# Attention and a maxout MoE on one core: states transposed by DMA, half of the weights multiplied pair by pair, and an earlier state transpose

## The chip, the cores and the metric

The kernel runs on one core of a Trainium2 chip. The metric is device time in microseconds (us). Before the change three runs gave 148.19, 148.46 and 148.90; the median is 148.46 us.

## What is computed

There are B = 8 batches of H = 8 heads, S = 512 positions of x, Ns = 32 states and D = 64. Attention runs both ways between x and the states; its output is one row per position (4352 rows, 512 wide), and each row goes through a maxout layer.

```python
scores = scale * x @ state.T                 # per batch and head: 512 x 32
xread  = softmax(scores) @ state             # 512 x 64
sread  = softmax(scale * state @ x.T) @ x    # 32 x 64
rows   = concat([xread, sread])              # all heads side by side: 544 x 512 per batch
h1, h2 = rows @ w1, rows @ w2                # 512 -> 1024
out    = maximum(h1, h2) @ w_out             # 1024 -> 512
```

Inputs and output are float32; the products are made in bfloat16.

## The kernel before, in words

**The algebra.** max(h1, h2) is relu(h1 - h2) + h2. So the kernel forms wd = w1 - w2 (`w_sub`) and wwo = w2 @ w_out (`w_wo_mm`, `w_wo_h_mm`), and since xread is the attention weights times the states, it multiplies the states of each batch by wd and wwo first: SW[b] = state x [wd, wwo] (`sw_mm`, `sw_two_mm`, `sw_h_mm`). A batch's rows are then relu(a x SW) x w_out plus a x SW: `l1_mm` and `l1_ev` (L1), `l2_f` and `l2_open` (L2), with `l2_out` copying to the output tile.

**The state matrices.** sbd holds, per batch, the states of head pairs as block-diagonal columns (4 pairs, 64 partitions for each of two heads). To fill it, states are cast to bf16 and transposed. Batches 0 and 1 have their own loads and transposes on TensorE (PE): `state_mm` (L132), then `state_ev` (two copies). Batches 2 to 7 share one load of 256 KB twice (`load_states`), one cast on GpSimd (POOL) into sbr (`states_cast`), eight PE transposes into one PSUM bank (`states_mm`, L157), and two copies of 64x768 (`states_ev`, one on ScalarE (ACT), one on VectorE (DVE)). A second way, `states_dma`, was in the file and was not called.

**Attention of a batch.** x is cast to xo (with a column of ones) and transposed to xt, for batch 0 in four head pairs (`cast_pair`, `xt_pair_mm`, `xt_pair_ev`), from batch 2 on by a DMA transpose of another cast xb (`cast_half`, `xt_dma`). Scores go through exp on ACT to e, DVE sums e to es and takes the reciprocal er (`reduce_pair`, `norm_sums`), and `norm_mul` (L294) multiplies e by er to give a, for one half (two of the four head pairs) at a time. `at_mm` (L317) transposes a on PE to aT for batches 0 and 1; from batch 2 on this is a DMA transpose. `sread_mm` makes the other direction.

**The weights.** w1, w2 and w_out are loaded in four pieces of 256 columns; piece 0 comes in two halves (`load_h`). On the way to wwo each piece of w2 is cast (`w2_cast`), transposed on PE (`w2_tr_mm`) and copied to w2t; each piece of w_out is cast to wo (`wo_cast`, `wo_cast_h` for the halves of piece 0). w1 halves are cast by `w1_cast_h`. The load of w2 piece 3 reuses the buffer of piece 0, and so waits for piece 0's subtraction.

**The order.** The kernel is under a manual schedule: each engine runs its instructions in the order in which the program writes them (lines 617 to 849), so that a waiting instruction holds up all behind it on its engine. Batch 0's attention, the weights' preparation, batch 0's L1 and L2 in parts, and batch 1's attention are interleaved by hand there; a loop over batches 1 to 7 follows, in which batch b's L1 and L2 run while batch b+1's attention is prepared. `idle(n)` (L572) issues n matmuls of 128x256 on a tile of zeros whose result nobody reads. SP issues nearly all DMAs, in written order. PSUM has two pools of four banks, pa and ps, of which a step gets a bank as its argument says.

**The steps around the change.** POOL's order before, in batch 0's part: cast of x pair 2, `state0_neg`, w2 half 0, `norm_mul(0,0)`, wo half 0 (line 648), w1 half 1 (line 655), `w_sub(0)` (line 671, L540), wo half 1 (line 677), w2 piece 1, wo piece 1. PE's order there: idle(15), transposes of x pair 0, idle(3), `state_mm(0)`, transposes of x pair 1, idle(3), scores of pair 0 and so on (lines 617 to 689). Around batch 1's end the lines are 786 to 836.

Of the kernel before, what the change touches and what calls it, by code (L numbers as in the profile page):

```python
# [15 lines left out]
def kernel(  # L16
# [9 lines left out]
    nc = tc.nc  # L26
    B, H, S, D = x.shape
    _, _, Ns, _ = state.shape
# [27 lines left out]
    def copy(eng, o, i):  # L56
        if eng == "A":
            nc.scalar.copy(o, i)  # L58
        elif eng == "V":
            nc.vector.tensor_copy(o, i)  # L60
        else:
            nc.gpsimd.tensor_copy(o, i)  # L62
# [61 lines left out]
    P = {}  # L124
# [5 lines left out]
    def state_mm(b, pool=None):  # L130
        p = P["st", b] = bank(BF16, pool)
        nc.tensor.transpose(p[:, 0:128], sb0[:, b], ident)  # L132
# [18 lines left out]
    def states_cast(eng):  # L151
        copy(eng, sbr.rearrange("p m j d -> p j m d"), sfr.rearrange("p j (m d) -> p j m d", m=8))

    def states_mm(pool=None):
        p = P["st"] = bank(BF16, pool)
        for m in range(8):
            nc.tensor.transpose(p[:, m * 128:(m + 1) * 128], sbr[:, m].rearrange("p j d -> p (j d)"), ident)  # L157

    def states_dma():
        P["st"] = xio.tile([128, NC * 256], BF16, tag="xb", name="stt")  # L160
        nc.sync.dma_start_transpose(out=P["st"].rearrange("p (m r) -> p m r", m=8), in_=sbr.rearrange("p m j d -> p (m j d)"))

    def states_ev(j, eng):
        o = sbd[64 * j:64 * j + 64, 2:B, :, 32 * j:32 * j + 32].rearrange("p b k (l m) -> p (b k) l m", l=4)
        copy(eng, o, P["st"][64 * j:64 * j + 64, :].rearrange("p (m k l) -> p k l m", m=8, l=4)[:, 8:])


    def cast_half(b, g, eng):
        if b not in st:
            st[b] = dict(xb=xio.tile([128, NC, H * D], BF16, tag="xb", name="xb"))  # L170
        copy(eng, st[b]["xb"][:, :, 256 * g:256 * g + 256].rearrange("p c (i d) -> p i c d", i=4),
             xf_t[b][:, 4 * g:4 * g + 4, :].rearrange("p i (c d) -> p i c d", c=NC))
# [15 lines left out]
    def cast_pair(b, k, eng, m=1):  # L188
        xo = st[b]["xo"]
        for j in range(k, k + m):  # L190
            copy(eng, xo[:, :, j, 2:130].rearrange("p c (i d) -> p i c d", i=2),
                 xf_t[b][:, 2 * j:2 * j + 2, :].rearrange("p i (c d) -> p i c d", c=NC))

    def xt_pair_mm(b, k, pool=None):
        d = st[b]
        if "xt" not in d:
            d["xt"] = at.tile([128, NC, 4, 128], BF16, tag="xt", name="xt")
        p = P["xt", k] = bank(BF16, pool)
        for c in range(NC):
            nc.tensor.transpose(p[:, c * 128:(c + 1) * 128], d["xo"][:, c, k, 2:130], ident)  # L200
# [11 lines left out]
    def scores_pair_mm(b, k, pool):  # L212
        d = st[b]
        if "e" not in d:
            att_tiles(b)
        p = P["sc", k] = bank(F32, pool)
        for c in range(NC):
            nc.tensor.matmul(p[:, c * 64:c * 64 + 64], d["xt"][:, c, k, :], sbd[:, b, k, :],
                             start=(c == 0), stop=(c == NC - 1))
# [10 lines left out]
    def xt_dma(b):  # L230
        d = st[b]
        d["xt"] = at.tile([128, NC, 4, 128], BF16, tag="xt", name="xt")
        nc.sync.dma_start_transpose(out=d["xt"].rearrange("p c k t -> p (c k) t"),
                                    in_=d["xb"].rearrange("p c m -> p (c m)"))
# [39 lines left out]
    def scores_ev(b, hh):  # L274
        ev = st[b]["e"].rearrange("p g c i n -> p (g c) i n")[:, :, 2 * hh:2 * hh + 2, :]
        nc.scalar.activation(out=ev.rearrange("p (g c) i n -> p g c (i n)", g=2),  # L276
                             in_=P["sc", hh].rearrange("p (c g m) -> p g c m", c=NC, g=2), func=ACTF.Exp, scale=scale)
# [5 lines left out]
    def norm_sums(b, hh, sums=True):  # L283
        d = st[b]
        if sums:
            ev = d["e"].rearrange("p g c i n -> p (g c) i n")[:, :, 2 * hh:2 * hh + 2, :]
            nc.vector.tensor_reduce(d["es"][:, hh], ev, axis=mybir.AxisListType.X, op=ALU.add)  # L287
        nc.vector.reciprocal(d["er"][:, hh], d["es"][:, hh])

    def norm_mul(b, hh, eng):  # L290
        d = st[b]
        ev = d["e"].rearrange("p g c i n -> p (g c) i n")[:, :, 2 * hh:2 * hh + 2, :]
        av = d["a"].rearrange("p g c i n -> p (g c) i n")[:, :, 2 * hh:2 * hh + 2, :]
        (nc.gpsimd if eng == "P" else nc.vector).tensor_mul(  # L294
            av, ev, d["er"][:, hh].unsqueeze(3).to_broadcast([128, 2 * NC, 2, Ns]))

    def norm(b, hh, eng, sums=True):
        norm_sums(b, hh, sums)
# [13 lines left out]
    def at_mm(b, g, pool=None):  # L312
        if b not in AT:
            AT[b] = keep.tile([128, 2, NC, 128], BF16, tag="at", name="aT")
        p = P["at", g] = bank(BF16, pool)
        for c in range(NC):
            nc.tensor.transpose(p[:, c * 128:(c + 1) * 128], st[b]["a"][:, g, c].rearrange("p i n -> p (i n)"), ident)  # L317

    def at_ev(b, g, eng):
        copy(eng, AT[b][:, g].rearrange("p c t -> p (c t)"), P["at", g][:, 0:512])  # L320
# [43 lines left out]
    def sw_ev(b, lo, hi, g, eng):  # L364
        copy(eng, SW[b][:, g, lo:hi], P["sw", b, lo][g][:, 0:hi - lo])
# [70 lines left out]
    def l2_open(b, c, p, start, stop):  # L436
        for g in range(2):
            nc.tensor.matmul(p, AT[b][:, g, c, :], SW[b][:, g, FF:WC], start=(start and g == 0), stop=(stop and g == 1))  # L438
# [6 lines left out]
    def l2_out(b, c, p, eng):  # L445
        if b not in OB:
            OB[b] = big.tile([128, NC, DM], F32, tag="ob", name="ob")
        copy(eng, OB[b][:, c, :], p)
# [62 lines left out]
    def w1_cast_h(j, eng):  # L511
        copy(eng, w1b[:, :, 128 * j:128 * j + 128], w1f[0][:, :, 128 * j:128 * j + 128])

    def wo_cast_h(j, eng):
        copy(eng, wo[:, j, :], wof[0][:, j, :])
# [23 lines left out]
    def w_sub(q, i0, i1, eng):  # L539
        (nc.gpsimd if eng == "P" else nc.vector).tensor_sub(  # L540
            wd[:, i0:i1, q * FQ:(q + 1) * FQ], w1f[q][:, i0:i1], w2f[q][:, i0:i1])
# [12 lines left out]
    def w_wo_h_mm(i, j, pool=None):  # L554
        if j == 0:
            P["wwo", 0, i] = bank(F32, pool)
        nc.tensor.matmul(P["wwo", 0, i], w2t[:, j, i, :], wo[:, j, :], start=(j == 0), stop=(j == 1))
# [10 lines left out]
    def idle(n, cols=256):  # L568
        if idle_p[0] is None:
            idle_p[0] = bank(F32, pa)  # L570
        for j in range(n):
            nc.tensor.matmul(idle_p[0][:, 0:cols], wz[:, 0:128], wz[:, 0:cols], start=True, stop=True)  # L572

    def l2_part(q, c):
        if ACC[c] is None:
            ACC[c] = bank(F32, pa)
        l2_f(0, c, ACC[c], (2 * q, 2 * q + 1), q == 0, False)
# [39 lines left out]
    idle(15)  # L617
    cast_pair(0, 0, "V")
    copy("A", sb0[:, 0], sf0[:, 0])
    xt_pair_mm(0, 0, pa)  # L620
    cast_pair(0, 1, "V")
    idle(3)
    state_mm(0, None)
    xt_pair_ev(0, 0, "V")
    xt_pair_mm(0, 1, pa)
    cast_pair(0, 2, "P")
    xt_pair_ev(0, 1, "V")
    state_ev(0, "A")
    idle(3)
    scores_pair_mm(0, 0, pa)  # L630
    cast_pair(0, 3, "V")
    xt_pair_mm(0, 2)
    xt_pair_ev(0, 2, "V")
# [11 lines left out]
    xt_pair_ev(0, 3, "A")  # L645
    idle(1)
    scores_pair_mm(0, 2, None)
    wo_cast_h(0, "P")
    scores_pair_ev(0, 2)
    reduce_pair(0, 2)  # L650
    idle(5)
    scores_pair_mm(0, 3, pa)
    scores_pair_ev(0, 3)
    w2_tr_h_mm(0)
    w1_cast_h(1, "P")
    w1_cast_h(0, "A")
    idle(3)
    sread_mm(0, pa)
# [1 line left out]
    sw_h_mm(0, pa)  # L660
    reduce_pair(0, 3)
    norm_sums(0, 1, False)
    norm_mul(0, 1, "V")
    w2_tr_h_ev(0, "A")
    sw_ev(0, 0, 128, 1, "A")
    idle(4)
    w_wo_h_mm(1, 0)
    at_mm(0, 0, pa)
    sw_ev(0, 0, 128, 0, "A")
    at_mm(0, 1)  # L670
    w_sub(0, 0, 4, "P")
    w_wo_h_mm(3, 0)
    w2_cast_h(1, "A")
    at_ev(0, 1, "V")
    sw_h_mm(1, pa)
    sw_ev(0, 128, 256, 1, "V")
    wo_cast_h(1, "P")
    w2_tr_h_mm(1)
    at_ev(0, 0, "A")
    l1_mm(0, 0)  # L680
# [103 lines left out]
    scores_mm(1, 1)  # L784
    l2_part(2, 2)
    states_cast("P")
    scores_ev(1, 0)
    cast_half(2, 0, "P")
    scores_ev(1, 1)
# [3 lines left out]
    sw_ev(0, FF, WC, 0, "A")  # L793
    norm_sums(1, 0)
    norm_mul(1, 0, "P")
    l2_part(3, 2)
    l2_part(3, 1)
    l2_part(3, 3)
    sw_mm(1, FF, WC)
    norm_sums(1, 1)  # L800
    sw_ev(1, FF, WC, 0, "A")
    sread_mm(1)
    norm_mul(1, 1, "P")
    l2_open(0, 3, ACC[3], False, True)
    l2_open(0, 2, ACC[2], False, True)
    l2_out(0, 3, ACC[3], "A")
# [1 line left out]
    at_ev(1, 0, "A")  # L808
    sw_ev(1, FF, WC, 1, "V")
    at_mm(1, 1)  # L810
    cast_half(2, 1, "P")
    sread_norm(1)
    states_mm()
    states_ev(1, "A")
    at_ev(1, 1, "V")
    cast_xo(2)
    l2_out(0, 2, ACC[2], "V")
    l2_open(0, 0, ACC[0], False, True)
    l2_open(0, 1, ACC[1], False, True)
    states_ev(0, "V")  # L820
    l2_out(0, 1, ACC[1], "A")
    l2_out(0, 0, ACC[0], "V")
    l1_mm(1, 6, pa)
    cast_half(3, 1, "P")
    l1_ev(1, 6, "A")
# [4 lines left out]
    l1_mm(1, 7)  # L830
    l1_mm(1, 1, pa)
    l1_mm(1, 3, pa)
    xt_dma(2)
    l1_ev(1, 5, "A")
    l1_ev(1, 0, "V")
    l1_mm(1, 2)
# [80 lines left out]
```

## Time and profile before

| | us |
|---|---|
| median of three runs | 148.46 |
| the profiled execution | 148.07 |
| its span (first to last instruction recorded) | 146.3 |
| PE busy in the span | 140.9 |
| DVE, ACT, POOL busy | 83.8, 69.5, 59.3 |
| idle matmuls (38), busy time | 7.9 |

The page counts an engine as busy while an instruction of it runs; matmuls overlap, so busy times of PE rows add up to more than their share of the span. The chain of work that ended last goes back from the last instruction to what released it, step by step: what does not stand in it has not set the end. The timeline lists instructions in order of time: start, duration, engine, line, operation, output and input, how many were merged, and in brackets the idle time before them with what ended it. PEld is PE's loading of weights, which runs beside the matmuls.

### The profile page before, as it was taken

Reading aid. Unit: us, or ns where it says so; the run is one execution under the profiler, and the core shown is the slowest. Engines: PE = TensorE matmul, PEld = TensorE weight load, DVE = VectorE, ACT = ScalarE, POOL = GpSimd, SP = SyncE. Lnnn points to the kernel's source line nnn. Section 1 sums busy time; section 2 is a strip of 40 time slices with the busy share of each in tenths; the row PEclk is TensorE's granted clock in tenths of the full one; section 3 lists DMA queues with packets and bytes.
Section 4 is the critical chain, followed back from the end, with each engine's and each line's share of the span. In section 5 each row is a group of like instructions: output and inputs, shape, how many; then the busy total and the mean of one; then the engine's idle time right before and its main releaser. Section 6 shows DMA issues by size and latency. Waiting matters only on the chain.

```text
span 146.3 us, 3237 instructions
## 1 busy us (share of the span) xinstructions
PE 140.9 (96%) x1314; PEld 71.5 (49%) x1314; DVE 83.8 (57%) x172; ACT 69.5 (47%) x135; POOL 59.3 (41%) x81
## 2 busy tenths in 40 slices
PE   6998999999999999999999999999999999999990
PEld 4764454364554445444544544454445344754460
DVE  3595695877874648464854675376557464621110
ACT  4387757686971456326450825271547135511110
POOL 2479435767948442925292347226500500000000
PEclk9999999999999999999999999999999999999999
DMA  3999999995459989496949685787306032402432
GB/s 126 308 321 351 356 362 362 361 350 165 93 104 338 211 286 283 81 270 246 242 85 286 251 184 109 250 297 138 72 36 251 8 73 121 166 4 72 143 121 94
DMA packets 36640, 29.18 MB, mean 199 GB/s; under 512 B 20241, under 2 KB 33809, under 8 KB 35729
## 3 DMA queue, kind: packets, MB, share of 16 engines
q1 hardware_dynamic: 36352, 28.91, 66.9%
q8 instruction: 10, 0.16, 0.4%
q10 hardware_dynamic: 272, 0.07, 0.2%
q14 instruction: 6, 0.04, 0.1%
HBM read 15.34 MB, written 8.91 MB: 166 GB/s over the span
## 4 chain that ended last, share of the span: by engine, by line
PE 91%; POOL 4%; DVE 2%; issue 0%; ACT 0%; POOLq 0%
PE acc L442 37%; PE ps L426 17%; PE acc L438 10%; PE ps L552 4%; PE acc L572 3%; PE ps L361 3%; PE ps L482 2%; PE acc L492 2%; PE ps L271 2%; POOL wd L540 2%; PE acc L328 1%; PE acc L466 1%; PE acc L490 1%; PE acc L426 1%; PE ps L533 1%; PE acc L361 1%
## 5 line engine op out<-in xcount | busy, mean ns | idle before, releaser
L442 PE MATMUL acc<-wo,r 128*128 128x512 bf16 x248 | 59.6, 379 | 0.0
L442 PEld LDWEIGHTS <-r 128*128 128x128 bf16 x248 | 23.8, 98 | 28.7 <-issue 0.6
L58 ACT COPY ob<-acc 128x512 f32<-128x512 f32 (+2 forms) x17 | 9.4, 554 | 48.8 <-PE acc L442 27.9
L426 PE MATMUL ps<-aT,sw 128*128 128x512 bf16 x118 | 27.9, 379 | 0.0
L294 POOL TENSOR_TENSOR a<-e,er 128x512 bf16<-128x512 bf16 x15 | 15.5, 1049 | 27.6 <-ACT e L276 20.3
L417 DVE TENSOR_SCALAR r<-ps 128x512 bf16<-128x512 f32 x26 | 18.0, 692 | 14.5 <-PE ps L426 14.4
L415 ACT ACTIVATE r<-ps 128x512 bf16<-128x512 f32 x33 | 19.7, 601 | 6.4 <-PE ps L426 5.7
L60 DVE COPY ob<-acc 128x512 f32<-128x512 f32 (+1 forms) x17 | 10.9, 644 | 16.3 <-PE acc L442 14.6
L426 PEld LDWEIGHTS <-sw 128*128 128x128 bf16 x128 | 12.2, 98 | 13.7
L62 POOL CAST xb<-xf 128x1024 bf16<-128x1024 f32 x12 | 12.4, 1040 | 15.1 <-DMA xf<-in_x_dram 15.1
L62 POOL CAST xo<-xf 128x512 bf16<-128x512 f32 x28 | 16.1, 615 | 5.8 <-DMA xf<-in_x_dram 5.4
L438 PE MATMUL acc<-sw,aT 128*128 128x512 bf16 x62 | 18.2, 380 | 0.0
L60 DVE CAST sw<-ps 128x512 bf16<-128x512 f32 x15 | 9.8, 687 | 12.0 <-PE ps L361 11.6
L58 ACT CAST sw<-ps 128x512 bf16<-128x512 f32 (+1 forms) x21 | 11.0, 573 | 2.9 <-PE ps L361 1.5
L287 DVE TENSOR_REDUCE es<-e 128x16 f32<-128x512 bf16 x14 | 9.2, 656 | 1.6 <-ACT e L276 1.6
L572 PE MATMUL acc<-wz 128*128 128x256 bf16 x38 | 7.9, 354 | 1.2 <-DVE ones L610 1.2
L276 ACT ACTIVATE e<-ps 128x512 bf16<-128x512 f32 x14 | 7.7, 597 | 0.8 <-PE ps L271 0.2
L438 PEld LDWEIGHTS <-aT 128*128 128x128 bf16 x62 | 5.0, 98 | 4.4
L552 PE MATMUL ps<-wo,w2t 128*128 128x512 bf16 x24 | 6.7, 380 | 0.0
L563 DVE TENSOR_TENSOR w2acc<-ps,w2acc 128x512 f32<-128x512 f32 x8 | 5.2, 686 | 1.7 <-PE ps L552 1.6
L572 PEld LDWEIGHTS <-wz 128*128 128x128 bf16 x38 | 4.3, 126 | 2.3 <-DVE ones L610 1.2
L540 POOL TENSOR_TENSOR wd<-w1f,w2f 128x1024 bf16<-128x1024 f32 x2 | 4.7, 2354 | 1.7 <-DMA w1f<-in_moe_w_dram 1.7
(109 smaller groups left out, 146.4 us busy)
## 6 DMA issues: line engine op xcount, KB each, us to landing
xf<-in_x_dram SPq DMA_DIRECT2D x14, 512.0 KB, 5.3
out_dram<-ob SPq DMA_DIRECT2D x7, 1024.0 KB, 4.2
w2f<-in_moe_w_dram SPq DMA_DIRECT2D x3, 512.0 KB, 8.1
w1f<-in_moe_w_dram SPq DMA_DIRECT2D x3, 512.0 KB, 9.1
wof<-in_moe_w_out_dram SPq DMA_DIRECT2D x3, 512.0 KB, 9.1
xf<-in_x_dram SPq DMA_DIRECT2D x4, 256.0 KB, 3.7
out_dram<-ob SPq DMA_DIRECT2D x3, 256.0 KB, 2.0
w2f<-in_moe_w_dram SPq DMA_DIRECT2D x2, 256.0 KB, 5.4
```

Source lines behind the costliest of these rows:

```text
L58: nc.scalar.copy(o, i)
L60: nc.vector.tensor_copy(o, i)
L62: nc.gpsimd.tensor_copy(o, i)
L287: nc.vector.tensor_reduce(d["es"][:, hh], ev, axis=mybir.AxisListType.X, op=ALU.add)
L294: (nc.gpsimd if eng == "P" else nc.vector).tensor_mul(av, ev, d["er"][:, hh].unsqueeze(3).to_broadcast([128, 2 * NC, 2, Ns]))
L415: nc.scalar.activation(out=o, in_=p, func=ACTF.Relu)
L417: nc.vector.tensor_scalar(o, p, scalar1=0.0, scalar2=None, op0=ALU.max)
L426: nc.tensor.matmul(p, SW[b][:, g, f * 128:(f + 1) * 128], AT[b][:, g].rearrange("p c t -> p (c t)"), start=(g == 0), stop=(g == 1))
L438: nc.tensor.matmul(p, AT[b][:, g, c, :], SW[b][:, g, FF:WC], start=(start and g == 0), stop=(stop and g == 1))
L442: nc.tensor.matmul(p, R[b][:, f, c * 128:(c + 1) * 128], wo[:, f, :], start=(start and j == 0), stop=(stop and j == len(fs) - 1))
L552: nc.tensor.matmul(p, w2t[:, f, i, :], wo[:, f, :], start=(f == fs[0]), stop=(f == fs[-1]))
L572: nc.tensor.matmul(idle_p[0][:, 0:cols], wz[:, 0:128], wz[:, 0:cols], start=True, stop=True)
```

## The change

In batch 0's part:

- The state transpose `state_mm(0)` goes ahead of the transposes of x pair 0. Of the idle matmuls, 3 before it become 1, 3 ahead of the scores of pair 0 become 1 behind them, and 5 ahead of the scores of pair 3 become 3.
- A new `norm_mul_pair` multiplies one head pair. Batch 0's second half, one multiply on DVE before, becomes pair 2 on POOL and pair 3 on DVE.
- On POOL the casts of wo half 0 and w1 half 1 move behind that multiply, and the cast of wo half 1 moves ahead of the subtraction `w_sub(0)`.
- On PE `w_wo_h_mm(1, 0)` moves behind the transposes of a, and changes PSUM pool with `at_mm(0, 0)`.

Around batch 1's end:

- `states_dma` takes the place of `states_mm`: SP issues a DMA transpose of sbr to a tile stt from the buffers of xb, right behind the cast. The two copies to sbd now read stt, and stand behind the output copies of batch 0.
- `norm_mul(1, 1)` goes from POOL to DVE, ahead of the copy `sw_ev(1, FF, WC, 1)`. On POOL `cast_half(2, 1)` moves up, right behind `norm_mul(1, 0)`, and on SP `xt_dma(2)` with it. On DVE `sread_norm(1)` moves behind the copy of aT.

```diff
+    def norm_mul_pair(b, k, eng):
+        d = st[b]
+        ev = d["e"].rearrange("p g c i n -> p (g c) i n")[:, :, k, :]
+        av = d["a"].rearrange("p g c i n -> p (g c) i n")[:, :, k, :]
+        (nc.gpsimd if eng == "P" else nc.vector).tensor_mul(
+            av, ev, d["er"][:, k // 2, :, k % 2].unsqueeze(2).to_broadcast([128, 2 * NC, Ns]))
...
     copy("A", sb0[:, 0], sf0[:, 0])
+    state_mm(0, None)
     xt_pair_mm(0, 0, pa)
     cast_pair(0, 1, "V")
-    idle(3)
-    state_mm(0, None)
+    idle(1)
     xt_pair_ev(0, 0, "V")
...
-    idle(3)
     scores_pair_mm(0, 0, pa)
+    idle(1)
...
-    wo_cast_h(0, "P")
     scores_pair_ev(0, 2)
     reduce_pair(0, 2)
-    idle(5)
+    idle(3)
     scores_pair_mm(0, 3, pa)
     scores_pair_ev(0, 3)
     w2_tr_h_mm(0)
-    w1_cast_h(1, "P")
...
-    norm_mul(0, 1, "V")
+    norm_mul_pair(0, 2, "P")
+    norm_mul_pair(0, 3, "V")
+    wo_cast_h(0, "P")
+    w1_cast_h(1, "P")
...
-    w_wo_h_mm(1, 0)
-    at_mm(0, 0, pa)
+    at_mm(0, 0)
     sw_ev(0, 0, 128, 0, "A")
     at_mm(0, 1)
+    w_wo_h_mm(1, 0, pa)
+    wo_cast_h(1, "P")
     w_sub(0, 0, 4, "P")
...
-    wo_cast_h(1, "P")
...
     states_cast("P")
+    states_dma()
...
     norm_mul(1, 0, "P")
+    cast_half(2, 1, "P")
...
     norm_sums(1, 1)
+    norm_mul(1, 1, "V")
     sw_ev(1, FF, WC, 0, "A")
     sread_mm(1)
-    norm_mul(1, 1, "P")
...
-    cast_half(2, 1, "P")
-    sread_norm(1)
-    states_mm()
-    states_ev(1, "A")
+    xt_dma(2)
     at_ev(1, 1, "V")
+    sread_norm(1)
     cast_xo(2)
...
-    states_ev(0, "V")
     l2_out(0, 1, ACC[1], "A")
+    states_ev(1, "A")
     l2_out(0, 0, ACC[0], "V")
+    states_ev(0, "V")
...
-    xt_dma(2)
```

More of the change, by code (lines that the diff above doesn't have):

```diff
@@ L810 @@
     at_mm(1, 1)
-    cast_half(2, 1, "P")
+    xt_dma(2)
+    at_ev(1, 1, "V")
     sread_norm(1)
-    states_mm()
-    states_ev(1, "A")
-    at_ev(1, 1, "V")
     cast_xo(2)
@@ L819 @@
     l2_open(0, 1, ACC[1], False, True)
+    l2_out(0, 1, ACC[1], "A")
+    states_ev(1, "A")
+    l2_out(0, 0, ACC[0], "V")
     states_ev(0, "V")
-    l2_out(0, 1, ACC[1], "A")
-    l2_out(0, 0, ACC[0], "V")
     l1_mm(1, 6, pa)
```

## The prediction

> **What bounds the kernel now.** I read four views in this order. First the page: TensorE (PE) is busy for 140.9 of 146.3 us.
>
> ```profile
> PE 140.9 (96%) x1314; PEld 71.5 (49%) x1314; DVE 83.8 (57%) x172; ACT 69.5 (47%) x135; POOL 59.3 (41%) x81
> DMA  3999999995459989496949685787306032402432
> ```
>
> So time goes only with PE work or PE gaps, and the loads fill the DMA engines for the first nine slices (33 us). Second, the chain of work that ended last, in order of time; its early part shows the only PE gaps.
>
> ```profile
> 10.29 1.08 POOL w1b L62
> 11.36 2.31 POOL wd L540
> 13.68 0.57 POOL wo L62
> 14.25 0.04 issue
> 14.29 0.38 PE ps L557
> ...
> 15.72 0.31 DVE sbd L60
> 16.02 0.04 issue
> 16.07 0.30 PE ps L361 x7
> ...
> 18.13 0.54 PE acc L442 x2
> 18.66 0.94 PE ps L552 x4
> ```
>
> The reader sees: until 14.29 the end is set by GpSimd (POOL), whose cast of the second half of w_out's first piece stands behind a 2.31 us subtraction; at 16.02 by the state copies on DVE; from 16.07 to the last matmuls at 142.76 every link is PE. Third, the timeline from 0 to 32 us for what stands around 18.6 us, where a gap could still hide.
>
> ```profile
> 10.93 0.62 ACT L58 CAST w2b<-w2f 128x512 bf16<-128x512 f32 x1 [0.17 <-DMA w2f<-in_moe_w_dram]
> ...
> 17.41 1.04 POOL L62 CAST wo<-wof 128x1024 bf16<-128x1024 f32 x1 [2.18 <-DMA wof<-in_moe_w_out_dram]
> 17.82 0.69 DVE L60 COPY w2t<-ps 128x1024 bf16<-128x1024 bf16 x1 [0.55 <-PE ps L533]
> ...
> 18.57 1.04 PE L552 MATMUL ps<-wo,w2t 128*128 128x512 bf16 x4
> ```
>
> The first product of the second weight piece (L552, 18.57) needs two things: w2t, ready at 17.82 + 0.69 = 18.51, and wo, ready at 17.41 + 1.04 = 18.45. The second hangs on a load that landed at about 17.4, and POOL stood idle 2.18 us for it. That load is a wall: however early PE comes, this product can't start before about 18.50. Fourth, the same chain from 36 to 43 us, where the other states are transposed.
>
> ```profile
> 37.00 0.45 PE ps L317 x8
> 37.44 0.45 PE ps L157 x8
> 37.89 0.86 PE acc L438 x4
> ...
> 42.32 0.47 PE ps L271 x16
> ```
>
> Here every step follows the last one on PE without a gap.
>
> **Part 1, the start: edits before 10 us.** Six idle matmuls go (3+3+5 become 1+1+3); the chain has three of them as 0.64 us before 6.8 us, and five between two others as about 0.5 us after it. The state transpose moves ahead of the first x transposes. They come 0.11 us later (one link "PE ps L132" of 0.11), but their copy on DVE started at 5.11, right behind the cast of pair 1, so this costs nothing. Scores of pair 0 come some 0.8 us earlier. The gain stops at the loads: the cast of pair 3 (DVE, 6.68) waits for the last quarter of x, issued at about 2.3 and landing 4.2 us later (the median of the last two of these four issues), at about 6.5. Behind that cast stand, unchanged, the transposes and exponentials of pairs 2 and 3. I take 0.1 us for the scale factors of the second half, bounds 0 and 0.4.
>
> **Part 2, the attention weights and POOL's order.** Before, DVE multiplies the second half in 1.04 us (9.86 to 10.90) while POOL casts; after, each engine takes one pair of 128x256, which no row shows. From the 128x512 rows (1.04 DVE, 1.05 POOL) half is 0.53; with nothing saved it would be 1.05. POOL's two casts beside DVE's multiply took 1.64 us (9.73 to 11.37) instead of 2 x 0.61 = 1.23, so POOL loses about 0.4 beside it; I take 0.8 for POOL's pair. It starts at about 9.97 (reciprocal ends 9.82, plus the 0.15 that the first multiply waited) and ends at 10.6 to 11.0; the transposes (10.95 before) then start at 10.7 to 11.05. Nothing is won behind them yet: ACT's copy of the first transposed half stands behind the cast that ends at 10.93 + 0.62 = 11.55, which waited for a DMA.
> The Trainium skill, "GPSIMD Engine Reference", section 1, says that POOL shares its SBUF interfaces with DVE and contends with DVE instructions that have two SBUF inputs. That speaks against running both halves at once: by it POOL's pair could end only after DVE's, at about 10.95, inside the bounds above, and nothing of the sum changes.
>
> POOL then casts wo half 0, w1 half 1, wo half 1 (0.61 each; their loads landed by 3.83+5.3 = 9.1, 4.38+5.6 = 10.0 and 5.41+6.3 = 11.7) and only then subtracts. wo half 1 is done at about 12.5 instead of 14.24, w1 half 1 at 11.9 instead of 11.37, the subtraction at 12.5 + 2.35 = 14.9 instead of 13.68. So the first L1 matmul comes about 0.25 later (12.4), but the product that stood until 14.29 goes at about 13.7: the gap closes. Then the states copies for batch 1 end at about 15.3, the wd matmuls start at about 15.2 instead of 15.74, PE is 0.6 us ahead (0.8 if POOL is undisturbed).
> What is queued behind the later subtraction: on POOL the cast w2 piece 1 (14.9 to 15.9; PE reads it at 16.96 before and about 16.5 after, slack 0.6); on SP the load of w2 piece 3, issued at 13.71 before, then at 14.9. At that time the queue still holds loads that landed up to 10.28 + 10.1 = 20.4, so the DMA engines do not run dry, and nothing lands later.
>
> **Where the 0.6 us go.** DVE's subtraction of piece 1 (16.05) can't move much: its load landed at 8.38 + 7.5 = 15.88. w2t is then ready at about 17.9, but wo stays at 18.45. PE, early, waits: 18.57 becomes 18.50. Of the front's 0.6 I keep **0.07 us**; the bounds are 0.8 (the whole gap) and a loss of 0.4 (rival b). From there PE ran without a gap, and its later loads (casts at 19.00, 21.98, 24.76, 26.66, 28.07) are ready 0.4 us or more ahead of their readers, so a shift of 0.07 meets none.
>
> **Part 3, the states.** Eight transposes leave PE: the link of **0.45 us**, in a stretch without gaps. In their place SP issues a DMA transpose of 256 KB once POOL's cast ends (31.90). No row shows it; the nearest are aT's, also 128x1024 bf16: 3.0 to 4.2 us to landing. The loads ahead of it run until 34.5 (333 GB/s from 31.9 to 34.5, 42 after), so I take a landing of 34.5 + 1.3 to 34.5 + 4.2, that is 36 to 38.7; the longest row in a full queue (10.1 us, a weight load) would give 42. Its copies on ACT and DVE move behind the output copies: ACT's starts at about 39.0, DVE's at about 39.8 (DVE: aT copy from 37.4, the two reciprocals and scales 0.67, two output copies 0.68 each) and ends at 40.8 if it still takes 0.95; that row reads PSUM, the new copy reads SBUF, and I bound it by 0.79 (ACT's row) and 1.35. The scores of batch 2 need it at 42.32 - 0.52 = 41.8. The L1 copies behind it shift by up to 0.4 on ACT and 0.7 on DVE; the last needed one frees a bank at about 42.1, read by PE at 42.27. Narrow, but it holds.
> The multiply of batch 1's second half goes from POOL (ended 36.30) to DVE (34.97 to 36.0), so its transposes at 37.0 are safe. POOL then casts x of batch 2 at 35.3 instead of 36.24; its DMA transpose goes out at 36.3 instead of 37.30. The two such rows here landed after 4.5 and 4.6 us: 40.9, against 41.8 needed; x of batch 3 gains too (40.9 instead of 41.77). All other batches are unchanged and PE-bound.
>
> **The sum.** 0.07 + 0.45 = 0.52 us. Against the profiled execution (148.07 us: span 146.3 and 1.77 around it) that is 147.55; the median of the three runs, 148.46, is 0.39 higher, and on it the sum gives 147.94. I predict **147.9**. A measurement of this kernel tells about 0.5% (0.74 us) from no change, so this is nominally "the same".
>
> **Rivals.** (a) The front's gain stays. If in the timed runs PE, not the load, sets 18.57, the whole 0.6 to 0.8 counts: 148.46 - 0.45 - 0.7 = 147.3. For it: the runs spread 148.19 to 148.90, and w2t at 18.51 was already later than wo, so whatever slows the front of other executions is absorbed by the new slack. Against it: POOL's 2.18 us wait for the load.
> (b) The start's clock. The rows give 0.64 us for three idle matmuls up to 6.8 us (213 ns each), then half of that, though the granted clock reads 1.00 throughout. Fewer idle matmuls could leave PE slow longer. The front has 0.55 us of slack, so I take no loss up to there; it would bring the time to 148.0 to 148.4, as would a DVE copy of the states that takes 0.4 us longer.
> The skill, "TensorE: Matmul & The Clock Gate", Part 1, has the clock freed after one busy window of about 3.4 us. By it a missed window would keep PE slow to about 10.1 us; by my estimate from that page the transposes then start near 11.3, still within the slack.
> (c) Slower: the states land late. ACT and DVE stop in their queues at the states' copies, and the L1 copies behind them hold PE's banks. This decides from a landing of about 39.9; at 41.0 (9.1 us after issue, as the states' own loads took 9.0 in the full queue) the copy of l1 6 ends at 42.4, that of l1 5 at 43.4, where PE wants its bank at 41.75: 1.65 us, 148.46 - 0.52 + 1.65 = 149.6. Against it: the queue is empty from 34.5.
> (d) The change does not do what it says: the transposes leave PE, but a DMA wait for x of batch 2 or a bank takes their place (0.45 given back): 148.4.
>
> **How the numbers follow.** Forecast 0.55 (147.6 to 148.2), (a) 0.25, (b) and (d) together 0.12, (c) 0.08. For the range I take (a) down to its full 0.8 + 0.45, 147.2, and up past (b) and (d) to 148.6; left out are (c) and edges. Faster by over 0.5%: (a) and a tenth from the forecast's lower edge, 0.35. Slower: (c), 0.08. Within: 0.57.
>
> **What would show it.** Right: the PE wait for POOL before 14.29 is gone; POOL's cast of piece 1 still starts at 17.4 behind the load, and PE waits for it up to 0.6 us; L157 gone and PE without a gap from 36 to 43 us; scores of batch 2 at about 41.8. Wrong: L552's first product well before 18.4 (then (a)); a PE wait at the scores of batch 2 or at a bank behind L58 or L60 (then (c), (d)); idle matmuls still at 213 ns after 7 us (then (b)).

## The result, and the profile after

| | before | after |
|---|---|---|
| median of six runs each, same chip | 148.66 us | 147.92 us |
| lowest, highest | 148.13, 148.92 | 147.80, 148.26 |
| the profiled execution | 148.07 | 148.26 |
| its span | 146.3 | 146.5 |
| PE busy in the span | 140.9 | 140.3 |

The ratio is 0.9958, interval [0.9934, 0.9982]: 0.4% faster, less than the 0.5% from which a measurement of this kernel tells a change from none. Executions that were disturbed as a whole are left out of the ratios here and below; the medians and counts of the experiments include them.

The forecast of 147.9 is met by the number. The traces don't carry its reasons, though. The profiled execution of after is the slowest of its six (the other spans are 146.0 to 146.2), and its span is no shorter than that of before although PE does 0.6 us less. First the page of after:

```profile
PE 140.3 (96%) x1300; PEld 70.3 (48%) x1300; DVE 84.3 (58%) x173; ACT 70.1 (48%) x135; POOL 59.6 (41%) x81
DMA  4999999999739999497958884777306032402422
```

The loads still fill the first nine slices. Then the chain of work that ended last, from 9.91 to the first product of weight piece 1 (L559 now, L552 before):

```profile
9.91 0.79 POOL a L301
10.70 0.55 POOL wo L62
11.25 0.39 POOL w1b L62
11.64 0.12 issue
11.76 0.61 POOL wo L62
12.37 2.31 POOL wd L547
14.68 0.98 POOL w2b L62
15.66 2.02 issue
17.68 0.02 POOLq L62
17.70 1.05 POOL wo L62
18.76 0.04 issue
18.80 1.02 PE ps L559 x4
```

PE and DVE have left the chain: it runs through POOL and then through 2.02 us in which POOL has nothing to do. What POOL waits for there stands in the timeline:

```profile
17.64 0.69 DVE L60 COPY w2t<-ps 128x1024 bf16<-128x1024 bf16 x1
17.67 0.41 PE L394 MATMUL ps<-wd,sbd 64*32 64x256 bf16 x16 [0.54 <-DVE wd L547]
17.70 1.04 POOL L62 CAST wo<-wof 128x1024 bf16<-128x1024 f32 x1 [2.04 <-DMA wof<-in_moe_w_out_dram]
...
18.80 1.02 PE L559 MATMUL ps<-wo,w2t 128*128 128x512 bf16 x4 [0.18 <-POOL wo L62]
```

The load of w_out piece 1 ends POOL's wait, and PE waits for POOL's cast. w2t is ready at 18.33 (18.51 before), wo at 18.74 (18.45 before, as this load landed 0.3 later). From the first product to the end the span has 127.70 us left, before 127.73: nothing behind it is won. The chain of after from 37 to 43 us, where the states' transposes were, shows why:

```profile
37.21 0.45 PE ps L324 x8
37.66 0.88 PE acc L445 x4
38.54 0.02 issue
38.56 0.58 ACT ob L58
39.15 0.02 issue
39.17 0.02 ACTq L422
39.18 1.55 ACT sbd L58
40.73 0.01 issue
40.75 1.58 ACT r L422 x3
42.33 0.04 issue
42.38 0.22 PE acc L353
42.59 0.47 PE ps L271 x16
```

The link of L157 is gone, and in its place the end passes through ACT for 3.8 us: an output copy, the states' copy, three L1 copies. The timeline of the same stretch names the wait:

```profile
39.17 1.56 ACT L58 COPY sbd<-stt 64x768 bf16<-64x768 bf16 x1
...
39.82 1.29 DVE L60 COPY sbd<-stt 64x768 bf16<-64x768 bf16 x1
...
42.38 0.22 PE L353 MATMUL acc<-ident,sr 128*128 128x128 bf16 x1 [0.34 <-ACT r L422]
...
42.43 0.63 PE L271 MATMUL ps<-sbd,xt 128*128 128x64 bf16 x16
```

L353 is the transpose of sread of batch 0 into a bank of pa, which ACT's third L1 copy frees at 41.72 + 0.60 = 42.32. PE was free for it at 42.38 - 0.34 = 42.04. Beside the wait of 0.34, the matmul behind it stands with 0.22 in the chain, where before has both transposes of sread in 0.11: together about the 0.45 that was to be won. The scores of batch 2 start 23.63 us after the first product, before 42.16 - 18.57 = 23.59.

### The profile page after: what moved, and what is told of

The parts are those of the page before. It is cut to its first block, busy times and chain, and to the rows that moved or that the text cites. A ratio compares the mean times of both kernels' runs of the same rounds, so it can differ in the third digit from the quotient of the medians.

```text
span 146.5 us, 3213 instructions
## 1 busy us (share of the span) xinstructions
PE 140.3 (96%) x1300; PEld 70.3 (48%) x1300; DVE 84.3 (58%) x173; ACT 70.1 (48%) x135; POOL 59.6 (41%) x81
## 4 chain that ended last, share of the span: by engine, by line
PE 83%; POOL 6%; DMA 3%; ACT 3%; issue 2%; DVE 1%; SPq 1%; POOLq 0%; ACTq 0%
PE acc L449 36%; PE ps L433 16%; PE acc L445 10%; PE ps L559 4%; DMA xf<-in_x_dram 3%; PE ps L368 3%; PE ps L489 2%; PE acc L499 2%; PE ps L271 2%; POOL wd L547 2%; POOL wo L62 2%; PE acc L335 1%; PE acc L473 1%; PE acc L497 1%; ACT r L422 1%
## 5 line engine op out<-in xcount | busy, mean ns | idle before, releaser
L294 POOL TENSOR_TENSOR a<-e,er 128x512 bf16<-128x512 bf16 x14 | 14.4, 1048 | 26.7 <-ACT e L276 19.2
L62 POOL CAST xb<-xf 128x1024 bf16<-128x1024 f32 x12 | 13.5, 1128 | 16.3 <-DMA xf<-in_x_dram 16.3
L60 DVE CAST sw<-ps 128x512 bf16<-128x512 f32 x15 | 9.8, 686 | 11.0 <-PE ps L368 10.6
L579 PE MATMUL acc<-wz 128*128 128x256 bf16 x32 | 6.8, 351 | 1.2 <-DVE ones L617 1.2
L559 PE MATMUL ps<-wo,w2t 128*128 128x512 bf16 x24 | 6.7, 379 | 0.2 <-POOL wo L62 0.2
L271 PEld LDWEIGHTS <-xt 128*128 128x128 bf16 x112 | 4.3, 98 | 2.1 <-issue 0.5
```

Of the source, the lines that this page charges most:

```text
L294: (nc.gpsimd if eng == "P" else nc.vector).tensor_mul(av, ev, d["er"][:, hh].unsqueeze(3).to_broadcast([128, 2 * NC, 2, Ns]))
L559: nc.tensor.matmul(p, w2t[:, f, i, :], wo[:, f, :], start=(f == fs[0]), stop=(f == fs[-1]))
```

## The experiments

Two theories stood against each other after the result. **F**: what the medians gained comes from the front, in executions whose loads come late; the states' 0.45 us are given back at ACT's copy. **S**: the states' 0.45 us are the gain, and the front gives about nothing, because of the load. In the expectations, Theory 1 is S; F is Theory 2 in e1 to e4 and Theory 3 from e9 on, and Theory 2 of e5 is that neither part gives anything. A table of the traces is at the end of this section.

**One part alone: e1_front_only, e2_states_only, and e4_before_again as a measure of the comparison.** e1 has the edits of batch 0's part and the order of before around batch 1's end:

```diff
-    states_dma()
...
+    states_mm()
+    states_ev(1, "A")
```

e2 is the reverse (DMA transpose and all moves around batch 1's end; idle matmuls, `norm_mul` and POOL's order of before). e4 is the kernel before under another name.

> Batch 0's part as after (state transpose first, fewer idle matmuls, pair multiply, POOL's order), the states of batches 2 to 7 as before, by eight transposes on PE. Theory 1 (the forecast: the front's gain ends at the load of w_out piece 1, worth 0.07 us; the rest is the transposes): 0.0 to 0.2 us below before, ratio 0.999 to 1.0. Theory 2 (from the traces: the transposes' 0.45 us is given back behind ACT's slower copy of the states, and the measured 0.7 us comes from the front): 0.5 to 0.8 below before, ratio 0.995 to 0.9965. In its trace PE has no wait for a bank between 38 and 43 us by both.

> The other half: batch 0's part as before, the states by DMA and the moves around batch 1's end as after. Theory 1: 0.4 to 0.5 us below before, ratio 0.9965 to 0.9975. Theory 2: within 0.15 of before, ratio 0.999 to 1.001; its trace has ACT's copy of the states at about 1.56 us and behind it a PE wait of about 0.3 us for a bank at the transposes of sread (L353 in the changed kernel), as in the trace of after.

> The kernel before, unchanged, for a second execution of it with a trace. By both theories ratio 0.998 to 1.002. Theory 1: w_out piece 1 and the first product of piece 1 (L552) stand within 0.1 us of each other, as in the first trace. Theory 2 (executions differ in the front): in an execution near 148.8 us L552's first product starts 0.3 us or more later than 18.57, and what it waits for is the row that names the cause.

Measured: e1 148.52, ratio 0.9987 [0.9959, 1.0016]; e2 148.59, 0.9996 [0.9978, 1.0014]; e4 148.41, 0.9995 [0.9972, 1.0019]. Neither part shows a gain by itself: F expected 0.995 to 0.9965 of e1, S 0.9965 to 0.9975 of e2, and both were missed. The interval of the control is as wide as what was sought. e1's profiled execution took 811.69 us, with 512-column matmuls at 1.32 us throughout and a granted clock of 1.00 in the records; it says nothing on the change. e2's trace says more: x pair 2 came at 6.92 in it, against 5.80 in that of before, and the front of before had no room for it:

```profile
17.40 1.64 POOL L62 CAST wo<-wof 128x1024 bf16<-128x1024 f32 x1 [1.31 <-DMA wof<-in_moe_w_out_dram]
18.69 0.69 DVE L60 COPY w2t<-ps 128x1024 bf16<-128x1024 bf16 x1 [0.55 <-PE ps L540]
...
19.43 0.55 PEld L559 LDWEIGHTS <-w2t 128*128 128x128 bf16 x4 [0.40 <-DVE w2t L60]
19.44 0.82 PE L559 MATMUL ps<-wo,w2t 128*128 128x512 bf16 x3
```

Here w2t, at 19.38, ends PE's wait and not the load: the product comes 0.87 late. Behind it, span minus start is 127.86, with 0.48 us of waiting at L353. In this execution that speaks for both halves of F.

**The bank: e3_states_pool, e5_after_again, e6_sread_later.** e3 takes the states' copy off ACT and gives it to POOL, behind `cast_xo(2)`. e6 leaves the copies alone and moves their victim, the transpose of sread of batch 0, behind the first output tile of batch 1. e5 is after under another name.

```diff
 # e3
-    states_ev(1, "A")
...
     cast_xo(2)
+    states_ev(1, "P")
 # e6
-    sread_tr_mm(0, pa)
-    sread_tr_ev(0, "V")
...
             l2(b, c)
+            if b == 1 and c == 0:
+                sread_tr(0, "V")
```

> The changed kernel with one copy of the states, ACT's, moved to POOL behind its casts of x for batch 2, so that ACT's queue has only the L1 copies there. Theory 1: as after, 147.9 (there is nothing to win back). Theory 2: PE's bank wait is gone, 0.3 to 0.45 below after: 147.45 to 147.6, ratio to before about 0.992 to 0.9935; batch 2's scores start 0.25 to 0.35 us ahead of where before has them, less what the load of w_out piece 1 lands later in that execution.

> The changed kernel once more, for a second trace and more runs beside e6 to e8. Theory 1 (the front's gain ends at the load of w_out piece 1; what is left of the 0.7 us are the transposes): ratio to before 0.996 to 0.998. Theory 2 (front and transposes each give next to nothing, as e1 and e2 read; the load's landing, which moves by 0.6 us between executions, sets the front): ratio 0.997 to 0.9995. In the trace by both: POOL's cast of w_out piece 1 starts when its load lands, and the first product of piece 1 0.05 us after the cast ends.

> The changed kernel with the transpose of batch 0's sread (the instruction at which PE waited 0.34 us for a bank behind ACT) and its copy moved into the loop, behind batch 1's first output tile; nothing else. If the give-back is that bank wait, batch 2's scores start 0.25 to 0.35 us earlier against the first product of piece 1 than in e5's trace, and the time is 0.2 to 0.4 below e5. If the wait only moves to the next bank that ACT frees late (that of batch 2's scores), within 0.1 of e5.

Measured: e3 149.64, 1.0090 [1.0059, 1.0122], slower; e5 148.06, 0.9971 [0.9942, 0.9999]; e6 147.97, 0.9954 [0.9928, 0.9981]. In e3 the scores of batch 2 start 41.50 - 18.37 = 23.13 us after the first product, so the 0.45 is there; but the copy on POOL (39.10, 1.51 us) pushes the casts of x of batch 3 behind it (39.39 in after, 40.67 here), and a DMA transpose soon after lands late. The chain of e3:

```profile
46.52 7.53 DMA aT<-a
...
54.08 3.61 PE ps L433 x16
```

The transpose of batch 2's a lands 7.53 us after its issue; in before such rows took 3.0 to 4.2. The issues just ahead of it are the transpose of x of batch 3, at 43.20, and an output store, at 44.63; whether these make it late wasn't tried apart. This is one way to lose 1.6 us (129.33 against 127.7) over a copy of 1.5 that no engine was short of time for. In e6, PE doesn't wait; the chain of e6:

```profile
41.49 0.43 PE ps L433 x2
41.92 0.06 PE acc L353
41.98 0.47 PE ps L271 x16
```

Scores after 23.08 us, span minus start 127.35: of the 0.45, about 0.35 stays. ACT's copy is as long as in after (39.12, 1.55 us). So the bank is what gave the 0.45 back. In the medians e5 and e6 cannot be told apart (0.1 us, where 0.2 to 0.4 was expected); the lowest time of twelve, 147.31, is 0.4 below e5's 147.71. e6 is the version to keep, for its trace.

**The load: e7_front_early, e8_before_early.** In both, `load_h(1, 0)` is left out, so one load of 256 KB fewer stands ahead of w_out piece 1. The front of after (states on PE), and before.

```diff
-        copy(eng, wo[:, j, :], wof[0][:, j, :])
+        copy(eng, wo[:, j, :], wof[0][:, 0, :])
...
-    load_h(1, 0)
```

> As e1 (batch 0's part as after, the transposes on PE), but the load of the second half of w_out's piece 0 (256 KB) is left out, and the first half is cast twice in its place, so that part of the weights is wrong; all later loads land about 0.7 us earlier. If the load of piece 1 is the wall that ends the front's gain (both theories): first product of piece 1 at 17.9 to 18.1, 0.5 to 0.6 below e1's time, ratio to before 0.995 to 0.9965. If something on the engines ends it, as e1: 0.998 to 0.9995.

> The kernel before with the same load left out (and the same wrong part). Its front is set by POOL's order and PE, so earlier loads give it little: first product of piece 1 at 18.45 to 18.57, ratio 0.999 to 1.0. If loads set it as well, 0.995 to 0.9965 as for e7.

Measured: e7 147.74, 0.9938 [0.9910, 0.9966]; e8 148.61, 0.9989 [0.9960, 1.0018]. With the load earlier, the front of after gains and before doesn't. The cast of piece 1 starts at 16.61 and 16.60, alike; in e7 the product comes at 18.12, behind w2t:

```profile
16.61 1.24 POOL L62 CAST wo<-wof 128x1024 bf16<-128x1024 f32 x1 [0.75 <-DMA wof<-in_moe_w_out_dram]
17.37 0.69 DVE L60 COPY w2t<-ps 128x1024 bf16<-128x1024 bf16 x1 [0.42 <-PE ps L540]
18.11 0.55 PEld L559 LDWEIGHTS <-w2t 128*128 128x128 bf16 x4 [0.40 <-DVE w2t L60]
18.12 1.04 PE L559 MATMUL ps<-wo,w2t 128*128 128x512 bf16 x4
```

So in after's front the load is a wall in these executions (in after wo is ready 0.4 us behind w2t), and in before it isn't what decides. e8's profiled execution, 2.1 us longer than e8's median, had x at 7.03 and the product at 19.56, and lost 1.6 us more before the scores of batch 2. Most of that went at a cast of w_out piece 2:

```profile
23.96 2.35 POOL L540 TENSOR_TENSOR wd<-w1f,w2f 128x1024 bf16<-128x1024 f32 x1 [1.73 <-DMA w1f<-in_moe_w_dram]
24.42 2.58 DVE L60 CAST wo<-wof 128x1024 bf16<-128x1024 f32 x1
...
27.06 1.04 PE L552 MATMUL ps<-wo,w2t 128*128 128x512 bf16 x4 [1.46 <-DVE wo L60]
```

In before this cast comes at 23.21, ahead of POOL's subtraction (24.76), and takes 0.69 us. Here it began 0.46 us behind the subtraction and ended 0.69 us after it, as if it had waited for it. So a front that comes late can cost more than its delay. Another 0.2 us went at the scores, which waited for the transpose of x, issued at 39.68 and landing 5.0 later. How often either happens, one trace doesn't show.

**A late x: e9_before_late, e10_after_late.** To make x late on purpose, a load of 256 KB goes ahead of the last two quarters of x, in before and in after:

```diff
+    load_h(0, 2)
     load_x(0, 4, 2)
     load_x(0, 4, 3)
-    load_h(0, 2)
```

> The kernel before with one load moved: the first half of w2's piece 0 (256 KB) is issued ahead of the third and fourth quarter of batch 0's x instead of behind them, so that these land about 0.7 us later and everything else at the same time. Theory 3 (from the traces: the third and fourth quarter of x landed anywhere from 5.7 to 7.0 us; before, the whole front hangs on them, so a late landing goes through to the end; after, the front has 0.5 us of slack ahead of the load of w_out piece 1, which takes it up): ratio to before 1.003 to 1.006; POOL's cast of x pair 2 at 6.5 to 7.2, first product of piece 1 at 19.1 to 19.5. Theory 1 (the loads of w_out set both): 0.999 to 1.001.

> The changed kernel with the same load moved. Theory 3: the slack takes most of the 0.7 us up, 0 to 0.3 us above the changed kernel (148.0 to 148.3), 0.6 to 0.9 us below e9; POOL's cast of x pair 2 at 6.5 to 7.2, first product of piece 1 at 18.5 to 18.9. If the front had no slack, it would lie 0.5 us or more above the changed kernel, as e9 above before.

Measured: e9 151.58 (six runs, 148.91 to 152.34), 1.0109 [1.0033, 1.0184] from two of them; e10 149.89 (twelve, 148.18 to 151.20), 1.0036 [0.9997, 1.0075] from eight. The delay was far larger than meant, 2.2 to 2.4 us and not 0.7, so that it uses up the slack of after as well, and the numbers expected of both were missed. The two profiled executions, each the longest of its runs, had x alike, as POOL's casts of e9 and e10 show, in this order:

```profile
8.24 0.61 POOL L62 CAST xo<-xf 128x512 bf16<-128x512 f32 x1 [6.79 <-DMA xf<-in_x_dram]
...
13.05 2.35 POOL L540 TENSOR_TENSOR wd<-w1f,w2f 128x1024 bf16<-128x1024 f32 x1
13.06 2.88 DVE L294 TENSOR_TENSOR a<-e,er 128x512 bf16<-128x512 bf16 x1
...
22.82 1.04 PE L552 MATMUL ps<-wo,w2t 128*128 128x512 bf16 x4
```

```profile
8.12 0.62 POOL L62 CAST xo<-xf 128x512 bf16<-128x512 f32 x1 [6.66 <-DMA xf<-in_x_dram]
...
20.85 1.04 PE L559 MATMUL ps<-wo,w2t 128*128 128x512 bf16 x4
```

At the first product after is ahead by 1.97 us; at the end by 1.1 (149.4 against 150.5), since e10 lost time behind it at DVE's cast of a later weight piece (25.30, 2.50 us in its chain), beside POOL's subtraction as in e8. But the 1.97 is not the slack of F. In e9 DVE's multiply fell beside POOL's subtraction and took 2.88 us, 1.84 more than in before; without that e9's product would stand at about 20.98, by an estimate from these rows, next to e10's 20.85. PE was slow for longer, too: idle matmuls still took 0.21 us each at 10.6 us in both (five in 1.07, three in 0.64), where from 7.1 us on they take half of that in before and after. So these two runs neither show nor refute F.

**The parts of the front: e11_front_again, e12_pool_only.** e11 repeats e1 under another name. e12 is the front without the earlier state transpose and with all idle matmuls of before: only POOL's order, the pair multiply and the move of `w_wo_h_mm`.

> As e1 (batch 0's part as after, the transposes of the states on PE), once more, since e1 gave no trace to read. Theory 3: the same gain as the whole change has, or up to 0.1 us less: ratio 0.996 to 0.9985; in its trace no wait of PE behind ACT at the transposes of sread, and batch 2's scores 23.6 us behind the first product of piece 1, as in before. If the transposes' 0.45 us is kept by the whole change, this one is 0.4 us slower than it.

> Of the front only POOL's new order and the multiply pair by pair (with the move of the product behind the transposes of a); idle matmuls, state transpose and the rest as before. Theory 3: the wait of PE for POOL (0.65 us) is gone with these alone, so as e11 within 0.1 us: ratio 0.9965 to 0.999. If the fewer idle matmuls and the early state transpose carry the gain: 0.999 to 1.001.

Measured: e11 148.37, 1.0005 [0.9976, 1.0033], where 0.996 to 0.9985 was expected: missed. e12 148.24, 0.9985 [0.9962, 1.0009]. Behind the first product their traces agree with the rest: span minus start 127.64 and 127.75. In e12 the product that waited for POOL until 14.29 in before follows the one at 13.32 without a wait, and the first of piece 1 comes at 18.45, for POOL's cast. e11's front shows what the new order costs:

```profile
12.81 0.62 POOL L62 CAST wo<-wof 128x512 bf16<-128x512 f32 x1 [0.65 <-DMA wof<-in_moe_w_out_dram]
13.38 2.35 POOL L547 TENSOR_TENSOR wd<-w1f,w2f 128x1024 bf16<-128x1024 f32 x1
...
18.76 1.02 PE L559 MATMUL ps<-wo,w2t 128*128 128x512 bf16 x4
```

The cast of wo half 1 now stands ahead of the subtraction, and here it waited 0.65 us for its load and started at 12.81, against 11.76 in after, with x as early as there (5.89). An earlier wait for w2 half 0 (8.65 instead of 7.52) had cost POOL the rest. So the subtraction began 1.05 us later than in after. The load of piece 1 was there at 17.26, which would allow a product at about 18.35 (an estimate: 1.04 for the cast and 0.05); it came at 18.76, when w2t (18.67) and POOL's cast (18.70, 1.44 us long) were done. In before that cast starts at 13.63, and a load that lands at 12.8 would hold up nothing. The front of after has more room for a late x and less for a late wo half 1.

Runs above 148.9, a rough mark for late ones: 25 of the 91 of before measured beside the experiments and two of e4's twelve; of the front alone 11 of 36 (e1 five, e11 five, e12 one); of the states alone (e2) two of twelve; of the whole change, e6 counted in, 3 of 30 (after and e6 none, e5 three). By this count the moves around batch 1's end go with fewer late runs at least as much as the front does. The chips differ from experiment to experiment and the counts are small, so this is a hint and no more.

**The traces side by side**, in us: the start of POOL's cast of x pair 2 (when x is there), of its cast of w_out piece 1, of the first product, and the span minus the latter.

| | x | w_out 1 | product | span minus product |
|---|---|---|---|---|
| before | 5.80 | 17.41 | 18.57 | 127.7 |
| e4 (before) | 6.03 | 17.09 | 18.55 | 127.8 |
| e2 (front of before) | 6.92 | 17.40 | 19.44 | 127.9 |
| after | 5.92 | 17.70 | 18.80 | 127.7 |
| e5 (after) | 6.67 | 17.67 | 18.76 | 127.7 |
| e12 (POOL's order) | 5.57 | 17.36 | 18.45 | 127.8 |
| e11 (front) | 5.89 | 17.26 | 18.76 | 127.6 |
| e7 (front, load early) | 5.67 | 16.61 | 18.12 | 127.8 |
| e6 (bank wait gone) | 6.14 | 17.65 | 18.75 | 127.4 |

The last column is the same with the states on PE and by DMA, except in e6. With a front of after and all loads the product column is 18.4 to 18.8, whether x comes at 5.6 or at 6.7; with that of before it goes from 18.6 to 19.4, the latter in one trace. e3, e8 and e10, which lose time further on, and e9 are not in the table.

## Why the prediction was right and wrong

**What bounds it now: right.** The load of w_out piece 1 is the wall of the front of after (POOL idle 2.04 us for it, and PE for POOL), and e7 moves the product when the load moves. It is not the wall in every execution: in e11 w2t and the length of POOL's cast decide.

**Parts 1 and 2: right.** The pair multiply on POOL took 0.79 (0.8 taken), the cast of wo half 1 ended at 12.37 (12.5), the subtraction at 14.68 (14.9), PE's wait of 0.65 for POOL is gone, wd's matmuls begin at 15.09 (15.2). What part 2 didn't ask is what a later load of wo half 1 does to the new order; e11 shows it. "Nothing lands later" wasn't so in the profiled execution: the load of w_out piece 1 came at 17.70 instead of 17.41, but between 17.1 and 17.7 over all traces, so that the change needn't be the cause.

**The term 0.07: right for executions like the profiled one, too small where x is late.** In the profiled one it measured nothing (18.80 against 18.57, because the load landed 0.3 later). But x comes between 5.6 and 7.0 from one execution to the next, and in e2, with x at 6.92, the front of before sets the product: 19.44, against 18.76 in e5, with x at 6.67. e5 had 0.11 us of room left (w2t ready at 18.60, wo at 18.71), so with e2's x it would have come at about 18.9, by an estimate. There the front is worth some 0.5 us, somewhat under the 0.6 to 0.8 of rival (a), and by the mechanism that (a) named. "Of the front's 0.6 I keep 0.07 us" took one execution for all; how often x is that late, the runs don't show.

**The term 0.45: wrong.** The transposes left PE, but the whole term came back, in both traces of the change and in e2's; rival (d) happened, with a bank. The step that failed is the end of part 3: "The L1 copies behind it shift by up to 0.4 on ACT ... the last needed one frees a bank at about 42.1, read by PE at 42.27. Narrow, but it holds." ACT's copy of the states was kept at its old 0.79; it took 1.56. The three L1 copies behind it (39.28, 39.78, 40.25 before) started at 40.75, 41.24, 41.72: 1.47 later, and the bank came free at 42.32. With 0.79 it would have been at 41.55, ahead of PE at 42.04. The bound of 1.35 from part 3 was given for DVE's copy, which took 1.29, and not for ACT's. The states landed at 31.86 + 7.3 = 39.16, later than the 36 to 38.7 of the prediction; as ACT was busy up to 39.14, this cost next to nothing (0.18 us of waiting in e2). e6 shows that without the bank wait 0.35 would be kept.

**The other steps of part 3** went as said in kind. POOL's cast of x of batch 2 began at 35.45 but took 1.50 instead of about 1.0 beside DVE's multiply (35.18, 0.88 us), so the DMA went out at 36.98 and not 36.3; it landed at 41.38 and nothing waited.

**Rival (b)** didn't come: the idle matmul at 7.14 takes 0.27 us in both traces. **Rival (c)** didn't either: the states were there 0.7 us ahead of the 39.9 from which it was to decide.

**So the sum** of 0.52 met the number by luck: 0.45 of it was given back, and the medians differ by 0.74 for other reasons (before has 148.66 over six runs, not 148.46). After and e5 show that both parts together give 0.3 to 0.4%, e2 that the states alone give nothing that can be told from noise. Where the gain comes from stays open. The front is the likely place by e2 and e5, but e1 and e11, the front alone, should then show after's gain, and show 0.9987 and 1.0005, with intervals that reach from 0.996 to 1.003. The other candidate is the order around batch 1's end, which sends out the transpose of x of batch 2 earlier (36.98 against 37.30) and may make late executions rarer, as the count of runs hints. No trace caught a late execution of e1 or e11, which could have told the two apart.

## What to carry to other kernels

When an operation moves off the bound engine, price what takes its place by its new source and its new place in a queue, and follow it to the next buffer or bank that the bound engine needs: here 0.77 us more on an engine that is half idle cost 0.45 us on PE. A front that hangs on loads should be judged over several executions, as a gain that one trace hides behind a load may be slack that other executions use; and a new order should be asked which load now holds up the rest (e11). An instruction that comes late can also meet a long one of another engine that it used to miss (e8). And where a wait is for a bank, moving the waiting step (e6) can be cheaper than relieving the engine that frees it (e3).

## What the runs showed of the hardware

- The copy of 64x768 bf16 took 0.79 us on ACT and 0.95 on DVE from PSUM, and 1.56 and 1.29 from stt in SBUF; on POOL 1.51, and DVE's part beside that took 1.88. Whether the source, its layout or the company makes the difference wasn't tried apart.
- Three DVE instructions that fell beside POOL's subtraction of 2.35 us took 2.58 (e8, cast), 2.49 (e10, cast) and 2.88 us (e9, multiply), instead of 0.69, 0.69 and 1.04 in before. The two casts ended 0.69 us after the subtraction did, the multiply 0.54.
- DMA transposes of 256 KB (aT) landed 3.0 to 4.2 us after their issue in before, those of 512 KB (x) 4.5 to 7.4; the one of the states, 256 KB behind weight loads, 7.3 in after, e2, e5 and e6, 6.6 in e10 and 5.9 in e3; one of aT 7.5 in e3, behind another transpose and a store.
- One load of 256 KB moved ahead of two quarters of x made x come 2.2 to 2.4 us later in the two profiled executions, though at the 319 to 363 GB/s that the page of after shows for the first slices it takes 0.7 to 0.8.
- The third quarter of x was ready between 5.57 and 7.03 us in executions with the same order of loads up to there, a larger spread than all that the change was to gain.
- POOL's cast of 128x1024 took 1.04 in most rows, and 1.50 beside a DVE multiply (35.45 in after), which itself took 0.88. POOL's multiply of 128x256 (0.79, 9.91 in after) ended 0.48 after DVE's (0.42, 9.80).
